# Maxima of the softmax turned on VectorE: neighbouring queries for the maximum pass of a pooled attention kernel

## The chip, the core and the metric

The kernel runs on one of the eight cores of a Trainium2 chip. Five engines work beside each other, each on its own instruction queue: TensorE (PE; its weight loads are listed apart as PEld), VectorE (DVE), ScalarE (ACT), GpSimd (POOL) and SyncE (SP), which in this kernel issues nearly all DMAs. The metric is the device time of one execution in microseconds (us), lower is better; the time before is the median of three executions.

## The reference

Attention with pooled queries (pairs of neighbouring queries averaged: 1152 become 576) over 8 batches of 8 heads with 64 dimensions, then a second stage on the result, x:

```python
q_pool = q.reshape(B, H, S // 2, 2, D).mean(axis=3)
scores = scale * np.matmul(q_pool, k.transpose(0, 1, 3, 2))
scores = scores - np.max(scores, axis=-1, keepdims=True)
attn = np.exp(scores)
attn = attn / (np.sum(attn, axis=-1, keepdims=True) + 1e-09)
x = np.matmul(attn, v)          # then laid out as (B, S/2, H*D)
theta = x @ w_theta
zr, zi = x * np.cos(theta), x * np.sin(theta)
u = x + einsum('ts,bsd->btd', w_tok_r, zr) + einsum('ts,bsd->btd', w_tok_i, zi)
out = u + np.maximum(u @ w_ch, 0.0)
```

The change touches only the way from the scores to `np.max(scores)`.

## The kernel before, in words

The first part of the program does the attention, in 32 pairs of heads (two heads of 64 dimensions fill the 128 partitions), and takes some 865 us; the second part does the rest batch by batch. In the first part each pair goes through these steps, and the steps of neighbouring pairs are interleaved:

- `prep_t`, `prep_hi`, `prep_lo`: TensorE turns keys and pooled queries (`pt`), ScalarE writes the rounded value `hi`, VectorE the rest `lo`. Both tiles hold, along a partition, the keys in two blocks with the 576 queries between them, from column `Q0` on.
- `maxpass` (line 317): the maximum of the scores is taken from `hi` alone. For each of four groups of 128 queries (`j`) and three groups of 384 keys (`g`) two matmuls, one per head, write `pm`. Here the 128 *queries* are the stationary operand, which TensorE loads before each matmul, and the keys stream past. VectorE reduces `pm` to a column of the small tile `mx` (line 324). A group `j` holds the queries j, j+4, j+8, ...: its columns stand four elements apart in `hi`. So twelve pairs of `pm` matmuls belong to one pair of heads. The last 64 queries go through `max_tail` (`px`, `py`).
- `max_nm` (line 345) makes `nm`, 128 partitions by 9 columns, the negated maxima: four columns for each head, and one for the tail.
- `load_max` (lines 351 and 352): four DMAs write `nm` into one row per head of `nmr`. With the spaced groups, partition p holds queries 4p to 4p+3 in four neighbouring words, so that a DMA writes 128 pieces of four words, or 64 of one word, to one partition.
- `escore` (line 371): eight matmuls write scores minus maximum into `pe` (three products of `hi` and `lo`, and `nmr` times a row of ones), ScalarE takes the exponential into `pc` (line 374). There are 18 of these per pair of heads.
- `ssum` (line 383): POOL adds the `pc` tiles of a half into `ss`, seven adds for each of two halves. TensorE sums `ss` over partitions (`pns`, line 419) and multiplies `pc` with the values (`pa`, line 397). The `norm_` steps divide, and turn the result (`xb`).

PSUM is used as four slots of two banks that `pm`, `pe`, `pt`, `px`, `pa`, `pns` share in turn. Tiles `ss` have two buffers per half, `pc` fourteen in all. The order of the instructions on every engine is written out: each step has a position in a table (`MAX_AT`, `PLAN`, `PREP_AT`), steps are sorted by position, and every engine, SP among them, runs its own in exactly that order. An instruction waits only for its own inputs and buffers, but everything behind it on its engine waits with it.

Of the kernel before, what the change touches and what calls it, by code (L numbers as in the profile page):

```python
# [9 lines left out]
F32 = mybir.dt.float32  # L10
F32R = mybir.dt.float32r
# [3 lines left out]
ALU = mybir.AluOpType  # L15
AX = mybir.AxisListType
# [68 lines left out]
def pooled_attention_moe_kernel(  # L85
# [11 lines left out]
    nc = tc.nc  # L97
    P = 128
    B, H, S, D = k.shape
    SQ = S // 2  # L100
    DM = H * D
    HALF = SQ // 2
    HT = SQ % P
    KC = SQ
    KT = S // P
# [39 lines left out]
    def bank2(kind, name):  # L145
        n = min(range(SLOTS), key=lambda k: slots[k])
        work, engines, after = HOLD[kind]
        psum["slot"] = n
        clock["p"] = max(clock["p"], slots[n]) + work
        end = max([clock["p"] + 0.3] + [clock[e] for e in engines]) + after  # L150
        for e in engines:
            clock[e] = end
        slots[n] = end + 0.1
        return psum["now"][0].tile([P, 2, 512], F32, tag=f"b{n}", name=name, bufs=1)
# [45 lines left out]
    with ExitStack() as p1:  # L200
# [7 lines left out]
        nrm = p1.enter_context(tc.tile_pool(name="nrm", bufs=1))  # L208
        sml = p1.enter_context(tc.tile_pool(name="sml", bufs=2))

        nmrs = [nrm.tile([P, 5 * P], F32R, name=f"nmr_{n}") for n in range(2)]
        for n in range(2):
            nc.gpsimd.memset(nmrs[n].bitcast(F32), 0.0)
        tails = [opd.tile([P, P], F32R, name=f"tail_{n}", bufs=1) for n in range(2)]
        for n in range(2):
            nc.gpsimd.memset(tails[n].bitcast(F32), 0.0)
        oner = nrm.tile([P, P], F32R, name="oner")
        nc.gpsimd.memset(oner.bitcast(F32), 0.0)
        for a in (0, D):
# [2 lines left out]
        state = {}  # L222
# [39 lines left out]
        Q0 = 6 * P  # L262
# [45 lines left out]
        def maxpass(i):  # L308
            st = state[i]
            hi = st["hi"]  # L310
            mx = st["mx"] = sml.tile([P, KT, 3], F32, tag="mx", name=f"mx{i}")
            W = 3 * P
            for j in range(4):
                for g in range(3):
                    pm = bank2("pm", f"pm{i}_{j}{g}")
                    for h, hs in enumerate(HEADS):
                        nc.tensor.matmul(  # L317
                            pm[:, h, 0:W],
                            hi[hs, Q0 : Q0 + 4 * P].rearrange("d (p j) -> d j p", j=4)[:, j],
                            hi[hs, K0[3 * g] : K0[3 * g] + W],  # L320
                            start=True,
                            stop=True,
                        )
                    nc.vector.tensor_reduce(  # L324
                        mx[:, j : j + 5 : 4, g : g + 1], pm[:, :, 0:W], AX.X, ALU.max
                    )
                    yield
# [13 lines left out]

        def max_nm(i):
            st = state[i]
            nm = st["nm"] = sml.tile([P, KT], F32R, tag="nm", name=f"nm{i}")
            nc.vector.tensor_reduce(nm, st["mx"], AX.X, ALU.max, negate=True)  # L345

        def load_max(i):
            nmr, nm = state[i]["nmr"].bitcast(F32), state[i]["nm"].bitcast(F32)
            for h in range(2):
                row = nmr[h * D : h * D + 1]  # L350
                nc.sync.dma_start(row[:, 0 : 4 * P], nm[:, 4 * h : 4 * h + 4])
                nc.sync.dma_start(row[:, 4 * P : SQ], nm[h * HT : (h + 1) * HT, 8:9])

        def escore(i, u, kt):
            st = state[i]
# [306 lines left out]
        def plan(i):  # L662
# [10 lines left out]
            for n, (name, fn, args) in enumerate((  # L673
# [4 lines left out]
                if i >= (3, 3, 3, 2, 2, 2, 2, 2)[n]:  # L678
                    at(base + PREP_AT[name], 3, fn, *args)
            at(base + pl["load_max"], 7, load_max, i)  # L680
            at(base + pl["load_v"], 5, load_v, i)
            gen = maxpass(i)
            for n in (MAX_AT0, MAX_AT1, MAX_AT)[min(i, 2)]:
                at(base + n, 2, run, gen, 1)
            at(base + pl["max_nm"], 7, max_nm, i)
            for u in range(2):
                for kt in range(KT):
# [366 lines left out]
```

## Time and profile before

| what | value |
|---|---|
| median of three executions | 1321.58 us (1321.48 to 1322.57) |
| the profiled execution: its own time, its span | 1321.95 us, 1320.2 us |
| PE busy, share of the span | 1288.2 us, 98% |
| PEld busy | 1083.3 us, 82% |
| POOL busy | 895.4 us, 68% |
| DVE busy | 847.7 us, 64% |
| ACT busy | 665.7 us, 50% |

The span is the time from the first to the last instruction of the program; the execution's own time is 1.75 us longer. A share is an average over both parts of the program: in forty equal slices of the span, POOL stands at 8 tenths or more from the third to the 26th, which is the first part, and mostly at 2 to 3 tenths after them. TensorE's granted clock is at nine tenths or more of full in all but the first slice.

### The profile page before, as it was taken

To read this page: it belongs to the slowest core of one execution; us is meant where nothing else is said; L and a number is where in the kernel's file an instruction comes from. 1 tells how busy PE (TensorE), PEld (TensorE's weight loads), DVE (VectorE), ACT (ScalarE), POOL (GpSimd) and SP (SyncE) were. 2 spreads that over 40 slices of the span, in tenths; PEclk is the share of its full clock that TensorE was granted. 3 is DMA by queue.
4 is the path that set the end of the run, shared out by engine and by line. 5 is a ranking of instruction groups with operands and counts; after the bars stand their busy time and mean duration, and the time that the engine had idled before them with its cause. 6 is when DMAs were issued, how large, how long until landed. Compare 5 with 4: busy or idle time off the path is not lost.

```text
span 1320.2 us, 29458 instructions
## 1 busy us (share of the span) xinstructions
PE 1288.2 (98%) x11850; PEld 1083.3 (82%) x11850; DVE 847.7 (64%) x1151; ACT 665.7 (50%) x1162; POOL 895.4 (68%) x664
## 2 busy tenths in 40 slices
PE   5999999999999999999999999999999999999998
PEld 3877787778787778787777777678899999999997
DVE  6766777676767686776777686545555636647452
ACT  1555555556565656565656555454443433434430
POOL 1799899999898998889998988834333333232310
PEclk7999999999999999999999999999999999999999
DMA  5335444444444444434544423225515335154231
GB/s 131 102 95 139 106 122 116 117 127 117 119 116 130 112 119 118 122 104 117 134 116 119 119 69 96 70 82 131 101 29 100 53 74 111 26 97 78 52 46 37
DMA packets 283209, 131.05 MB, mean 99 GB/s; under 512 B 247024, under 2 KB 247152, under 8 KB 283072
## 3 DMA queue, kind: packets, MB, share of 16 engines
q1 hardware_dynamic: 282896, 128.71, 40.0%
q8 instruction: 93, 1.52, 0.5%
q0 software_dynamic: 176, 0.46, 0.1%
q14 instruction: 44, 0.36, 0.1%
HBM read 97.21 MB, written 30.70 MB: 97 GB/s over the span
## 4 chain that ended last, share of the span: by engine, by line
PE 89%; DVE 4%; ACT 3%; DMA 1%; issue 1%; POOL 1%; SPq 0%; POOLq 0%; ACTq 0%; DVEq 0%
PE pe L371 21%; PE pa L397 21%; PE py L874 15%; PE pm L317 8%; PE pr L913 7%; PE pth L786 7%; PE pt L277 4%; PE pns L419 3%; DVE mx L324 2%; PE px L334 1%; ACT pc L374 1%; ACT Z L843 1%; DMA kn<-in_k_dram 0%; DMA xn<-xbd 0%; PE pwt L600 0%
## 5 line engine op out<-in xcount | busy, mean ns | idle before, releaser
L383 POOL TENSOR_TENSOR ss<-ss,pc 128x576 f32<-128x576 f32 x376 | 548.5, 1459 | 33.0 <-ACT pc L374 7.7
L324 DVE TENSOR_REDUCE mx<-pm 128x2 f32<-128x768 f32 x384 | 358.4, 956 | 204.6 <-PE pm L317 204.5
L374 ACT ACTIVATE pc<-pe 128x576 f32<-128x576 f32 x576 | 344.7, 652 | 79.1 <-PE pe L371 64.2
L397 PE MATMUL pa<-pc,vn 128*64 128x288 f32 x2304 | 294.1, 409 | 0.0
L397 PEld LDWEIGHTS pa<-pc,vn 128*64 128x64 f32 x2304 | 160.1, 137 | 119.1 <-DVE nm L345 7.4
L874 PE MATMUL py<-wtk,Z 128*128 128x288 f32 x1728 | 233.4, 295 | 0.0
L874 PEld LDWEIGHTS py<-wtk,Z 128*128 128x128 f32 x1728 | 231.9, 189 | 1.3
L847 POOL TENSOR_TENSOR Z<-ab,Z 128x512 fp32r<-128x512 f32 x40 | 52.1, 1303 | 257.3 <-ACT Z L843 242.0
L317 PE MATMUL pm<-hi 64*128 64x384 f32 x768 | 174.0, 464 | 4.7 <-ACT hi L293 2.1
L371 PE MATMUL pe<-hi 64*128 64x288 f32 x1152 | 174.1, 296 | 2.9 <-ACT pc L374 1.7
L371 PE MATMUL pe<-nmr,oner 64*128 64x288 f32 x1152 | 172.2, 292 | 1.6 <-DMA nmr<-nm 1.6
L371 PE MATMUL pe<-lo,hi 64*128 64x288 f32 x1152 | 172.2, 293 | 0.0
L371 PE MATMUL pe<-hi,lo 64*128 64x288 f32 x1152 | 172.1, 293 | 0.0
L317 PEld LDWEIGHTS pm<-hi 64*128 64x128 f32 x768 | 118.2, 306 | 35.3 <-issue 26.0
L409 ACT COPY xu<-pa 128x288 f32<-128x288 f32 x64 | 25.5, 399 | 212.9 <-PE pa L397 212.9
L371 PEld LDWEIGHTS pe<-hi 64*128 64x128 f32 x1152 | 113.6, 192 | 7.2 <-ACT pc L374 2.6
L383 POOL TENSOR_TENSOR ss<-pc,pc 128x576 f32<-128x576 f32 x64 | 92.3, 1442 | 31.9 <-ACT pc L374 31.6
L371 PEld LDWEIGHTS pe<-nmr,oner 64*128 64x128 f32 x1152 | 110.6, 185 | 2.0 <-DMA nmr<-nm 1.9
L371 PEld LDWEIGHTS pe<-hi,lo 64*128 64x128 f32 x1152 | 110.2, 185 | 0.0
L371 PEld LDWEIGHTS pe<-lo,hi 64*128 64x128 f32 x1152 | 110.0, 185 | 0.0
L913 PEld LDWEIGHTS pr<-us,wch 128*128 128x128 f32 x768 | 104.2, 189 | 1.7
L913 PE MATMUL pr<-us,wch 128*128 128x288 f32 x768 | 105.1, 295 | 0.0
(99 smaller groups left out, 1499.5 us busy)
## 6 DMA issues: line engine op xcount, KB each, us to landing
qn<-in_q_dram SPq DMA_DIRECT2D x32, 576.0 KB
kn<-in_k_dram SPq DMA_DIRECT2D x64, 288.0 KB
vn<-in_v_dram SPq DMA_DIRECT2D x32, 576.0 KB
dn<-ro SPq DMA_DIRECT2D x64, 144.0 KB
xd<-xu SPq DMA_DIRECT2D x32, 288.0 KB
xbd<-xb SPq DMA_DIRECT2D x32, 288.0 KB
xT<-xd SPq DMA_DIRECT2D x8, 1152.0 KB
xn<-xbd SPq DMA_DIRECT2D x140, 64.0 KB
```

The source lines that it names most:

```text
L277: nc.tensor.transpose(out=pt[:, n, c : c + R], in_=src.rearrange("p h d -> p (h d)"), identity=ident[0:R, 0:R],)
L317: nc.tensor.matmul(pm[:, h, 0:W], hi[hs, Q0 : Q0 + 4 * P].rearrange("d (p j) -> d j p", j=4)[:, j], hi[hs, K0[3 * g] : K0[3 * g] + W], sta ...
L324: nc.vector.tensor_reduce(mx[:, j : j + 5 : 4, g : g + 1], pm[:, :, 0:W], AX.X, ALU.max)
L371: nc.tensor.matmul(pe[:, h, 0:HALF], w[hs], x[hs], start=(n == 0), stop=(n == 3))
L374: nc.scalar.activation(pcs[u, kt], pe[:, :, 0:HALF], AF.Exp, scale=SC)
L383: nc.gpsimd.tensor_tensor(st["ss", u], first, st["pc"][u, kt], ALU.add)
L397: nc.tensor.matmul(pa[hs, 0, 0:HALF], st["vn"][:, h, kt, :], st["pc"][u, kt][:, h, :], start=(kt == 0), stop=(kt == KT - 1),)
L419: nc.tensor.matmul(px[a : a + 32, 1, 0:HALF], ones, sets[u][n][:, h, :], start=(n == 0), stop=(n == len(sets[0]) - 1), tile_position=(0, a),)
L786: nc.tensor.matmul(th, xs[c][:, j * P : (j + 1) * P], ws[:, c], start=(n == 0), stop=(n == 11))
L847: engine("zlo", b).tensor_tensor(Z[1], t, Z[0].bitcast(F32), ALU.subtract)
L874: nc.tensor.matmul(st["py", c, u][:, 0:HALF], Z[zi][:, c * P : (c + 1) * P], wtk[wi][:, kw, u * HALF : (u + 1) * HALF], start=(i == 0 and ...
L913: nc.tensor.matmul(pr[u][:, 0:HALF], wch[wi][:, c, e * P : (e + 1) * P], st["us", ui][:, c, u * HALF : (u + 1) * HALF], start=(n == 0), st ...
```

## The change

Three things change. The groups of queries in `maxpass` are now 128 neighbouring ones (0 to 127, 128 to 255, ...), so that the stationary operand is a plain slice of `hi`. The column of a group then holds the maxima of neighbouring queries down the partitions, so `max_nm` writes the nine columns into a tile `nm` of 32 columns that is kept (single, cleared once at the start), and VectorE turns it in four 32x32 pieces into `nt`, nine rows of 128. And `load_max` copies rows of `nt`: four rows of 128 words, and one row of 64, per head. `nmr` is 64 columns narrower.

```diff
-        nmrs = [nrm.tile([P, 5 * P], F32R, name=f"nmr_{n}") for n in range(2)]
+        nmrs = [nrm.tile([P, SQ], F32R, name=f"nmr_{n}") for n in range(2)]
...
+        TB = 32
+        nm = nrm.tile([P, TB], F32, name="nm")
+        nc.vector.memset(nm, 0.0)
+        nt = nrm.tile([TB, P], F32, name="nt")
...
                         nc.tensor.matmul(
                             pm[:, h, 0:W],
-                            hi[hs, Q0 : Q0 + 4 * P].rearrange("d (p j) -> d j p", j=4)[:, j],
+                            hi[hs, Q0 + j * P : Q0 + (j + 1) * P],
                             hi[hs, K0[3 * g] : K0[3 * g] + W],
...
         def max_nm(i):
             st = state[i]
-            nm = st["nm"] = sml.tile([P, KT], F32R, tag="nm", name=f"nm{i}")
-            nc.vector.tensor_reduce(nm, st["mx"], AX.X, ALU.max, negate=True)
+            nc.vector.tensor_reduce(nm[:, 0:KT], st["mx"], AX.X, ALU.max, negate=True)
+            for g in range(0, P, TB):
+                nc.vector.transpose(nt[:, g : g + TB], nm[g : g + TB])
 
         def load_max(i):
-            nmr, nm = state[i]["nmr"].bitcast(F32), state[i]["nm"].bitcast(F32)
+            nmr = state[i]["nmr"].bitcast(F32)
             for h in range(2):
                 row = nmr[h * D : h * D + 1]
-                nc.sync.dma_start(row[:, 0 : 4 * P], nm[:, 4 * h : 4 * h + 4])
-                nc.sync.dma_start(row[:, 4 * P : SQ], nm[h * HT : (h + 1) * HT, 8:9])
+                nc.sync.dma_start(row[:, 0 : 4 * P], nt[4 * h : 4 * h + 4])
+                nc.sync.dma_start(row[:, 4 * P : SQ], nt[8:9, h * HT : (h + 1) * HT])
```

The order of instructions is the same on PE, ACT, POOL and SP; only VectorE's has new rows. On VectorE, in the middle of the first part (sixteenth pair of heads; the numbers after a name only tell buffers apart), the queue before reads:

```order
L324 TENSOR_REDUCE mx_5584<-pm_32_5914 128x2
L345 TENSOR_REDUCE nm_5943<-mx_5584 128x9
L468 TENSOR_TENSOR xu_5174<-xu_5174,dn_5777 128x576
L473 STREAM_TRANSPOSE xb_5948<-xu_5174 128x576
L304 TENSOR_TENSOR lo_5714<-pt_16_5918,hi_5713 128x960
```

and now:

```order
L328 TENSOR_REDUCE mx_5632<-pm_32_5962 128x2
L348 TENSOR_REDUCE nm<-mx_5632 128x9
L350 STREAM_TRANSPOSE nt<-nm 32x32 x4
L473 TENSOR_TENSOR xu_5219<-xu_5219,dn_5825 128x576
L478 STREAM_TRANSPOSE xb_5999<-xu_5219 128x576
L308 TENSOR_TENSOR lo_5762<-pt_16_5966,hi_5761 128x960
```

Four 32x32 pieces stand behind `nm` and ahead of the division and the `lo` of the next pair; nothing else moved. On SP, for the same pair of heads, the queue before reads (`rd` and `rc` are DMAs of the division, `qn` loads queries):

```order
L436 DMA rd_6031<-sm_5940 4x288
L351 DMA nmr_117<-nm_5943 1x128x4
L352 DMA nmr_117<-nm_5943 1x64x1
L351 DMA nmr_117<-nm_5943 1x128x4
L352 DMA nmr_117<-nm_5943 1x64x1
L442 DMA rc_6071<-rd_6031 128x9
```

and now:

```order
L441 DMA rd_6082<-sm_5988 4x288
L356 DMA nmr_117<-nt 1x4x128
L357 DMA nmr_117<-nt 1x16x4
L356 DMA nmr_117<-nt 1x4x128
L357 DMA nmr_117<-nt 1x16x4
L447 DMA rc_6122<-rd_6082 128x9
```

The four DMAs keep their places; only their source and the pieces that they move are others.

## Rows read from the trace of the kernel before

**Rows 1.** Page, busy us (share) xinstructions; and the chain that ended last, by line.
```profile
PE 1288.2 (98%) x11850; PEld 1083.3 (82%) x11850; DVE 847.7 (64%) x1151; ACT 665.7 (50%) x1162; POOL 895.4 (68%) x664
...
PE pe L371 21%; PE pa L397 21%; PE py L874 15%; PE pm L317 8%; PE pr L913 7%; PE pth L786 7%; PE pt L277 4%; PE pns L419 3%; DVE mx L324 2%; PE px L334 1%; ACT pc L374 1%; ACT Z L843 1%; DMA kn<-in_k_dram 0%; DMA xn<-xbd 0%; PE pwt L600 0%
```
**Rows 2.** Page, groups: form xcount | busy us, mean ns of one | idle before.
```profile
L317 PE MATMUL pm<-hi 64*128 64x384 f32 x768 | 174.0, 464 | 4.7 <-ACT hi L293 2.1
...
L317 PEld LDWEIGHTS pm<-hi 64*128 64x128 f32 x768 | 118.2, 306 | 35.3 <-issue 26.0
...
L371 PEld LDWEIGHTS pe<-hi,lo 64*128 64x128 f32 x1152 | 110.2, 185 | 0.0
```
**Rows 3.** Timeline of PE: start us, us, instruction, xcount, idle before.
```profile
401.73 0.29 PE L371 MATMUL pe<-nmr,oner 64*128 64x288 f32 x2
401.86 0.44 PE L317 MATMUL pm<-hi 64*128 64x384 f32 x2
402.14 0.30 PE L371 MATMUL pe<-hi 64*128 64x288 f32 x2
...
414.99 0.56 PE L317 MATMUL pm<-hi 64*128 64x384 f32 x2
415.39 0.30 PE L371 MATMUL pe<-hi 64*128 64x288 f32 x2
```
**Rows 4.** Groups of PE by form, two widths of the same kind of matmul.
```profile
L874 PE MATMUL py<-wtk,Z 128*128 128x288 f32 x1728 | 233.4, 295 | 0.0
...
L786 PE MATMUL pth<-wth,xh 128*128 128x512 f32 x288 | 74.1, 400 | 2.2 <-DVE r L812 2.1
```
**Rows 5.** Waits of the weight loads: us in total, times, longest us.
```profile
PEld pm L317 <- issue: 26.0, 60, 0.4
```
**Rows 6.** Timeline of PE, a score tile directly behind the value matmuls.
```profile
832.62 0.40 PE L371 MATMUL pe<-hi 64*128 64x288 f32 x2
832.85 0.29 PE L371 MATMUL pe<-lo,hi 64*128 64x288 f32 x2
```
**Rows 7.** Timeline of VectorE, the first pair's maxima.
```profile
13.21 10.46 DVE L324 TENSOR_REDUCE mx<-pm 128x2 f32<-128x768 f32 x12
```
**Rows 8.** Windows from one pns to a next: us, busy PE PEld DVE ACT POOL.
```profile
252.79:278.90 26.11, 26.03 (x276) 20.40 (x276) 18.33 (x24) 14.79 (x26) 25.48 (x19) 1.00 0.46 124
278.90:305.18 26.28, 26.12 (x276) 20.50 (x276) 20.75 (x25) 15.15 (x27) 24.68 (x19) 1.00 0.51 126
305.18:331.49 26.31, 26.31 (x281) 20.93 (x281) 18.64 (x21) 14.75 (x26) 23.16 (x18) 1.00 0.39 103
...
409.37:436.04 26.67, 26.11 (x276) 20.50 (x276) 17.55 (x22) 15.48 (x28) 25.30 (x20) 1.00 0.43 122
...
sum 757.66, PE 754.01 PEld 595.23 DVE 545.92 ACT 438.61 POOL 695.25; mean PE 26.00 PEld 20.53 DVE 18.82 ACT 15.12 POOL 23.97
```
**Rows 9.** Groups of VectorE by form.
```profile
L473 DVE STREAM_TRANSPOSE xb<-xu 128x576 f32<-128x576 f32 x32 | 24.9, 779 | 2.1 <-DMA xbd<-xb 1.0
...
L345 DVE TENSOR_REDUCE nm<-mx 128x9 fp32r<-128x27 f32 x32 | 5.7, 180 | 0.9
...
L125 DVE MEMSET eps<- 128x1 f32 x1 | 0.1, 59 | 0.0
```
**Rows 10.** Timeline of VectorE behind two nm.
```profile
311.41 0.96 DVE L324 TENSOR_REDUCE mx<-pm 128x2 f32<-128x768 f32 x1 [1.02 <-PE pm L317]
...
410.09 0.18 DVE L345 TENSOR_REDUCE nm<-mx 128x9 fp32r<-128x27 f32 x1
...
415.60 1.82 DVE L324 TENSOR_REDUCE mx<-pm 128x2 f32<-128x768 f32 x2 [1.95 <-PE pm L317]
```
**Rows 11.** Timeline of SP: issue of two DMAs of maxima.
```profile
29.92 0.61 SPq L352 DMA_DIRECT2D nmr<-nm  x1
...
411.85 0.53 SPq L351 DMA_DIRECT2D nmr<-nm  x1
```
**Rows 12.** Timeline of PE, the first use of the maxima.
```profile
31.43 0.94 PE L371 MATMUL pe<-nmr,oner 64*128 64x288 f32 x2 [1.59 <-DMA nmr<-nm]
```

## The prediction

> **What bounds the kernel now.** I read the page first, for shares and the chain; then the groups, for what one instruction costs; then TensorE's timeline in the middle of the first part, for what a matmul costs in its place; then windows by pair of heads, for who is next behind TensorE; last the waits, VectorE's and SP's. TensorE is busy 98% of the span, and the chain that ended last runs over PE lines nearly throughout [rows 1]. In the first part it hardly waits: the 29 pairs of heads from 69.33 to 826.99 us take 757.66 us, and TensorE is busy 754.01 of them [rows 8]. So what shortens TensorE's work there shortens the kernel, until another engine is late. That would be POOL, busy 695.25 us of the same stretch, 92%; VectorE has 72%, ScalarE 58%.
>
> The line that the change touches, `pm`, stands out in one respect. Its weight load, 64 rows by 128 columns, takes 306 ns; that of `pe` has the same shape, reads the same tile `hi`, and takes 185 [rows 2]. The difference that I see in the code is that the columns of the first stand four elements apart. Loads run under the matmuls before them, so one must see whether the 121 ns come out. They do: `pm` starts 0.13 us behind a `pe` (401.73 to 401.86), which is what any `pe` takes, and the next `pe` comes only 0.28 us later [rows 3].
>
> **The change part by part.** *The load.* What a `pm` pair (two matmuls, one per head, side by side) would take if its load were hidden: 0.13 us as a `pe` of 288 columns, plus 96 more columns. A matmul of 512 columns takes 400 ns and one of 288 takes 295 [rows 4], 0.47 ns a column, so 45 ns more, 0.175 us together. It takes 0.28: the gain is 0.105 us. This also fits the 0.121 us that the load itself should lose, less what was hidden.
>
> Sixty of the `pm` pairs start behind a `pa`, where the load finds nothing to hide under: it is 60 times that the load engine stood idle before them [rows 5]. There `pm` to next `pe` takes 0.40 us [rows 3]. A `pe` directly behind a `pa` takes 0.23 [rows 6], and with 0.045 for the columns 0.275: the gain is 0.125.
>
> There are 768 matmuls, 384 pairs [rows 2]. The twelve of the first pair of heads gain nothing: VectorE's twelve maxima stand end to end for 10.46 us there and set the pace [rows 7]. I also leave out the next three, in the same start-up. So 309 x 0.105 = 32.4 us, and 60 x 0.125 = 7.5 us: TensorE's work gets 39.9 us shorter, 1.3 us for each pair of heads. All of it lies on the chain, if nothing takes its place. Its lower bound is 0 (a rival below); above it I allow nothing, since the `pm` would then be faster than its columns.
>
> *What is late next.* The repeating pattern is seven pairs of heads long, and POOL's share differs in it, since the preparation of the weights for the second part comes in some of them. In the window 252.79 to 278.90 POOL is busy 25.48 of 26.11 us, and the 0.63 us between its instructions look like all that it can't use. TensorE would then want 26.03 - 1.3 = 24.73. POOL can't follow: the pair lasts 0.75 us longer (POOL busy without a break) to 1.38 (with its breaks). The next window wants 26.12 - 1.3 = 24.82 against POOL's 24.68, even; the third wants 25.01 against 23.16, so POOL catches up; that of 409.37 wants 24.81 against 25.30, 0.49 to 1.12 us short, but behind lighter pairs [rows 8]. The sums say that POOL just fits on average: 695.25 + 29 x 0.63 = 713.5 us against TensorE's 754.01 - 29 x 1.3 = 716.3. Only the unevenness costs. Lower bound 0, if two buffers of `ss` and fourteen of `pc` level it all; upper bound, nothing levelled, 1.38 + 0.49 + 1.12 = 2.99 us in seven pairs, 12.4 us over 29. I take 1.2 us in seven, the one heaviest pair nearly whole, since the others have a lighter one ahead: 5 us.
>
> *The pieces.* VectorE gets 4 x 32 = 128 turns of 32x32. The trace has none so small. The bounds are 59 ns, the shortest instruction on VectorE, and 779 ns, a whole turn of 576 columns [rows 9]; by columns a piece has an eighteenth of that one, and `nm` itself, 27 columns in, takes 180. I take 0.1 us, nearest to the small rows: 0.4 us for a pair of heads, and some 0.1 for the wait on `nm`. Behind them on VectorE stand the division of an older pair, its turn, the `lo` of the next pair, and the first maxima of that pair. There VectorE waits for TensorE anyway, 1.95 us at 415.60 and 1.02 at 311.41 [rows 10]; so 0.5 us cost nothing, and `lo` is first read several us later. If that idle were gone, the price would be 0.5 x 31 = 16 us.
>
> The first piece waits for `nm`, and for the DMAs that read `nt` for the pair before, since `nt` is single. Those were issued some 26 us earlier, one pair of heads, so I count nothing.
>
> *The DMAs.* The four keep their place in SP's queue. `nm` ends at 410.27 [rows 10] and the first of them is issued at 411.85 [rows 11], behind other DMAs: the half microsecond of turning falls into a wait that is there. Only in the first pair of heads does TensorE wait for them, 1.59 us until 31.43 [rows 12], the last being issued at 29.92 to 30.53 [rows 11]. Fewer pieces could shorten this by anything from 0 to 1.6 us, a later `nt` could lengthen it by 0.5; I take 0.5 us less.
>
> Sum: -39.9 + 5 + 0 - 0.5 = -35.4 us, against the profiled execution's 1321.95 us (span 1320.2): 1286.5. The median of the runs is 0.4 lower, 1321.58: **1286 us**.
>
> **The rivals.** *POOL as the bound throughout.* If each pair keeps POOL's breaks, and its adds don't level out over the buffers, 12.4 us go instead of 5, and 1321.6 - 39.9 + 12.4 = 1294 us; with TensorE's slots freed a little later too, up to 1300. For it speaks the 92%; against it that a pair in three has over 1.5 us to spare. Chance 0.20. *POOL costs nothing:* 1321.6 - 39.9 - 0.5, some 1281 us, with all of the first wait gone 1280. For it speak the averages above; against it the window in which POOL is full. Chance 0.10.
>
> *The load doesn't get shorter.* Then nothing changes on TensorE, and the pieces are covered: 1322 us, within 0.2% of before. For it speaks only that the 306 ns come with `pm` and could hang on something else in it, such as its 384 moving columns; against it that the load of `pe`, same tile and shape, has 185. Chance 0.05. The Trainium skill, "TensorE: Matmul & The Clock Gate", section "LDWEIGHTS (loading the stationary operand)", says that a load takes as long as its number of columns, which by its words would give both loads the same time and the change no gain. The 306 and 185 ns of two loads of 128 columns [rows 2] speak against it here. "SBUF — State Buffer" of the Trainium skill, section "Door 1: The DMA port swizzle (why `[64,N]` ≈ `[32,N]`)", has reads lose speed where each falls into another line of 16 bytes; a step of four words does just that, and by that rule the gain is the one worked out above.
>
> *VectorE's queue behind `nm`*, the case that is slower. Four pieces of d us stand ahead of `lo` and of the next maxima. Past 1.95 / 4 = 0.49 us a piece they eat the idle of VectorE behind them, the slots of `pm` come free later, and TensorE waits; past (1.95 + 1.3) / 4 = 0.81 us they eat more than the load gives. The whole turn of 576 columns takes 0.779 [rows 9], so this needs pieces no cheaper than that and a load that gains little: without gain 31 x (3.12 - 1.95) = 36 us, 1358 us. Chance 0.02.
>
> **How the numbers follow.** Forecast 0.63, POOL throughout 0.20, POOL free 0.10, load unchanged 0.05, VectorE 0.02. The range takes in the free case's 1280 and most of POOL's case: 1279 to 1298. About 0.2%, 2.6 us, is what a measurement of this kernel can tell from no change. Faster by more: the first three, 0.93, and a little of the fourth, where the first wait gets shorter, 0.94; within: 0.03; slower: 0.03, the last case and a share of the fourth with costly pieces.
>
> **What would show it.** The load of `pm` near 185 ns, and 0.17 to 0.18 us from a `pm` to the next `pe` in the middle of the first part; the 29 pairs of heads some 34 us shorter, with POOL busy 96% or more of them, and TensorE idle where POOL's `ss` or a `pc` buffer is late, most in the windows with the weights' preparation; pieces below 0.2 us, with VectorE still idle behind them; the second part as long as before. I am wrong in the load if it stays near 306, in the price of POOL if TensorE is idle for less than 2 us or more than 12 in that stretch beyond what it is now, and in the cover if VectorE's idle ahead of the next maxima is gone.

## The result, and the profile after

The changed kernel takes 1302.34 us (median of four runs, 1300.03 to 1302.37) against 1321.8 of the kernel before beside it: ratio 0.9848, 95% interval 0.9831 to 0.9865. So it is 19.5 us faster, and not the 35.4 us that were forecast. 1302.34 lies above the whole range of 1279 to 1298. Timed a second time, beside two of the experiments below, it took 1302.12 (1301.99 to 1302.93), ratio 0.9858 (0.9841 to 0.9874).

The page of its profile, busy time (share of the span) xinstructions, and the chain that ended last by line; these answer to [rows 1].

```profile
PE 1264.4 (97%) x11850; PEld 1044.2 (80%) x11850; DVE 878.0 (68%) x1280; ACT 669.5 (51%) x1162; POOL 896.2 (69%) x664
...
PE pe L376 22%; PE pa L402 21%; PE py L879 15%; PE pr L918 8%; PE pth L791 7%; PE pm L321 5%; PE pt L281 4%; PE pns L424 3%; DVE mx L328 2%; ACT pc L379 1%; PE px L338 1%; DVE lo L308 1%; DVE xu L473 1%; ACT Z L848 1%; DVE wf L547 1%
```

Line `pm` has gone from 8% of the chain to 5%, `pe` stays on top, and three lines of VectorE, `lo`, `xu` and `wf` (preparation of the weights), are new in it with 1% each. TensorE's busy time has dropped by 23.8 us. By shares alone nothing has come up behind it.

The groups of the page, as in [rows 2]: busy, mean ns of one | idle before.

```profile
L376 PE MATMUL pe<-hi 64*128 64x288 f32 x1152 | 185.6, 316 | 8.1 <-DVE lo L308 2.7
L376 PE MATMUL pe<-nmr,oner 64*128 64x288 f32 x1152 | 173.0, 293 | 1.0 <-DMA nmr<-nt 1.0
L376 PE MATMUL pe<-lo,hi 64*128 64x288 f32 x1152 | 172.0, 292 | 0.0
...
L321 PE MATMUL pm<-hi 64*128 64x384 f32 x768 | 137.5, 368 | 4.4 <-ACT hi L297 2.1
...
L376 PEld LDWEIGHTS pe<-hi 64*128 64x128 f32 x1152 | 109.8, 185 | 23.3 <-DVE lo L308 4.5
...
L321 PEld LDWEIGHTS pm<-hi 64*128 64x128 f32 x768 | 73.8, 188 | 37.9 <-issue 25.1
```

The weight load of `pm` takes 188 ns, as that of `pe`; it was 306. The matmuls of `pm` take 368 instead of 464. So the load did what was forecast. The row that betrays the loss is the first: of the four products that make a score tile, the first one, `pe<-hi`, has a mean of 316 ns, and the other three 292 or 293. Before, it was 296, and the others 292 or 293:

```profile
L371 PE MATMUL pe<-hi 64*128 64x288 f32 x1152 | 174.1, 296 | 2.9 <-ACT pc L374 1.7
```

Its weight load in the changed kernel is as short as theirs. Something lengthens the first matmul of a tile, and it counts as busy time, not as idle.

The timeline of PE at the place of [rows 3], in the middle of the first part: start, us, instruction.

```profile
392.99 0.29 PE L376 MATMUL pe<-nmr,oner 64*128 64x288 f32 x2
393.12 0.34 PE L321 MATMUL pm<-hi 64*128 64x384 f32 x2
393.29 0.30 PE L376 MATMUL pe<-hi 64*128 64x288 f32 x2
...
393.69 0.29 PE L376 MATMUL pe<-nmr,oner 64*128 64x288 f32 x2
393.82 0.39 PE L376 MATMUL pe<-hi 64*128 64x288 f32 x2
394.05 0.29 PE L376 MATMUL pe<-lo,hi 64*128 64x288 f32 x2
```

From the `pm` to the next `pe` it is 0.17 us (393.12 to 393.29), where it was 0.28. But at the second score tile behind this `pm`, the `pe<-hi` at 393.82 lasts 0.39, and the next product comes 0.23 us behind it instead of 0.13. That is 0.1 us lost, as much as the `pm` has won. The same place before:

```profile
402.54 0.30 PE L371 MATMUL pe<-nmr,oner 64*128 64x288 f32 x2
402.67 0.30 PE L371 MATMUL pe<-hi 64*128 64x288 f32 x2
402.81 0.29 PE L371 MATMUL pe<-lo,hi 64*128 64x288 f32 x2
```

The weight loads of the changed kernel around that tile:

```profile
393.56 0.19 PEld L376 LDWEIGHTS pe<-nmr,oner 64*128 64x128 f32 x2
393.81 0.19 PEld L376 LDWEIGHTS pe<-hi 64*128 64x128 f32 x2
393.92 0.19 PEld L376 LDWEIGHTS pe<-lo,hi 64*128 64x128 f32 x2
```

In the first and the third row a load starts 0.13 us ahead of its own matmul (393.69 and 394.05) and lies under the matmuls before it. The second one should start at 393.69 and starts at 393.81, beside its own matmul. It waited, and with nothing to lie under it its time comes out. The Trainium skill ("TensorE: Matmul & The Clock Gate", section "Architectural detail: the array is 16× 32×32, not 1× 128×128") says that TensorE's queue can pull loads ahead of matmuls in flight; the row at 393.56 agrees, and that at 393.81 shows a load that was not pulled ahead.

What it waited for is seen on VectorE:

```profile
392.80 1.83 DVE L328 TENSOR_REDUCE mx<-pm 128x2 f32<-128x768 f32 x2
```

Two maxima stand here in one row; the first starts at 392.80, takes 0.96 and ends at 393.76, 0.05 us before that load starts. It frees the PSUM slot of the `pm` that started at 392.31, four slots back, and the tile at 393.82 is the next in that slot. The written order of the program says the same, here in two of its rows near a `pm 12`:

```
L376 MATMUL pe_02_5834<-hi_4974 128x288 [waits Activation_49]
...
L376 MATMUL pe_03_5848<-hi_4974 128x288 [waits DVE_49]
```

Half of the 18 score tiles follow a score tile in their slot and wait for ScalarE's exponential (the first row's tile follows a `pa` and waits for ScalarE's copy). The fourth, eighth, tenth, 14th and 18th of a pair of heads follow a `pm` and wait for VectorE, and the 12th follows a `pt` (each in 26 or 27 of 27 pairs of heads). For the eighth and the fourth the times can be read one by one, counted from the start of the `pm` that had the slot (medians of 27 pairs of heads, us, from the starts and ends in the timelines of PE, PEld and VectorE):

| | kernel | reduction ends | load of the new tile starts | its matmul starts | load ahead of its matmul |
|---|---|---|---|---|---|
| 8th tile | before | 1.44 | 1.49 | 1.61 | 0.12 |
| 8th tile | after | 1.34 | 1.39 | 1.40 | 0.01 |
| 4th tile | before | 1.57 | 1.62 | 1.74 | 0.12 |
| 4th tile | after | 1.45 | 1.50 | 1.51 | 0.01 |

The load starts 0.054 us behind the end of the reduction, in both kernels: it waits for VectorE, and did so before. But before, the four slots took 1.61 us to come round (two `pm` with two score tiles between them), and the load still had its 0.12 us ahead of its matmul. In the changed kernel the `pm` shorten the round by 0.21 us, and the reduction's end by 0.10 only. So the load comes out from under the matmuls: the tile's first product waits for it, which is the 0.1 us.

Over 27 pairs of heads, what the second product of a tile came later than 0.133 us behind the first, summed by place of the tile (worked out from the starts in TensorE's timeline, us; the changed kernel by its second profile):

| tile of the pair of heads | 4th | 8th | 10th | 12th | 14th | 18th | all 18 |
|---|---|---|---|---|---|---|---|
| before | 0.07 | 0.09 | 0.01 | 0.21 | -0.02 | 0.38 | 1.12 |
| after | 2.66 | 2.12 | 0.46 | 0.94 | 1.59 | 2.48 | 10.93 |

The windows from one `pns` to a next answer to [rows 8]: us, busy time of PE, PEld, DVE, ACT, POOL.

```profile
247.55:273.68 26.13, 25.28 (x277) 19.08 (x276) 20.47 (x29) 14.87 (x26) 25.50 (x20) 1.00 0.45 124
...
sum 739.72, PE 731.28 PEld 558.59 DVE 571.75 ACT 442.01 POOL 696.09; mean PE 25.22 PEld 19.26 DVE 19.72 ACT 15.24 POOL 24.00
```

The 29 pairs of heads take 739.72 us instead of 757.66, 17.9 less (the forecast was 34). TensorE is idle for 8.4 us of them, before 3.65. What it waited for in this stretch, us in total, times, longest:

```profile
PE pe L376 <- DVE lo L308: 2.7, 4, 1.0
PE pe L376 <- ACT pc L379: 2.1, 4, 0.7
PE pe L376 <- DVE mx L328: 1.9, 4, 0.5
```

POOL does not stand in it, though in the window of 247.55 it is busy 25.50 of 26.13 us. VectorE does, 4.6 us, twice: for a late `lo`, and for maxima. One of the four late `lo`, on VectorE:

```profile
95.23 0.18 DVE L348 TENSOR_REDUCE nm<-mx 128x9 f32<-128x27 f32 x1
95.44 0.84 DVE L350 STREAM_TRANSPOSE nt<-nm 32x32 f32<-32x32 f32 x4
96.32 1.80 DVE L473 TENSOR_TENSOR xu<-xu,dn 128x576 f32<-128x576 f32 x1
98.16 0.78 DVE L478 STREAM_TRANSPOSE xb<-xu 128x576 f32<-128x576 f32 x1
98.86 1.12 DVE L308 TENSOR_TENSOR lo<-pt,hi 128x960 fp32r<-128x960 f32 x1
```

and on TensorE:

```profile
100.03 0.40 PE L376 MATMUL pe<-hi 64*128 64x288 f32 x2 [1.03 <-DVE lo L308]
```

At the same place before:

```profile
94.95 0.87 DVE L542 SCALAR_TENSOR_TENSOR wf<-raw,wf 128x513 uint32<-128x513 uint32 x1
96.82 0.88 DVE L468 TENSOR_TENSOR xu<-xu,dn 128x576 f32<-128x576 f32 x1
```

The four turns take 0.84 us together, with `nm` ahead and the division and its turn behind, and `lo` ends after TensorE wants it. But the division takes 1.80 us here and took 0.88 before, and a `wf` among the last maxima takes 1.40 instead of 0.87. In both kernels the division takes anything from 0.74 to over 3 us; what sets that stays open, so the lateness is not the turns' alone.

### The profile page after: what moved, and what is told of

The parts are those of the page before. It is cut to its first block, busy times and chain, and to the rows that moved or that the text cites. A ratio compares the mean times of both kernels' runs of the same rounds, so it can differ in the third digit from the quotient of the medians.

```text
span 1300.6 us, 29614 instructions
## 1 busy us (share of the span) xinstructions
PE 1264.4 (97%) x11850; PEld 1044.2 (80%) x11850; DVE 878.0 (68%) x1280; ACT 669.5 (51%) x1162; POOL 896.2 (69%) x664
## 4 chain that ended last, share of the span: by engine, by line
PE 86%; DVE 6%; ACT 3%; issue 2%; DMA 1%; POOL 1%; SPq 0%; POOLq 0%; ACTq 0%; DVEq 0%
PE pe L376 22%; PE pa L402 21%; PE py L879 15%; PE pr L918 8%; PE pth L791 7%; PE pm L321 5%; PE pt L281 4%; PE pns L424 3%; DVE mx L328 2%; ACT pc L379 1%; PE px L338 1%; DVE lo L308 1%; DVE xu L473 1%; ACT Z L848 1%; DVE wf L547 1%
## 5 line engine op out<-in xcount | busy, mean ns | idle before, releaser
L379 ACT ACTIVATE pc<-pe 128x576 f32<-128x576 f32 x576 | 348.4, 652 | 62.7 <-PE pe L376 39.5
L376 PE MATMUL pe<-hi 64*128 64x288 f32 x1152 | 185.6, 316 | 8.1 <-DVE lo L308 2.7
L321 PE MATMUL pm<-hi 64*128 64x384 f32 x768 | 137.5, 368 | 4.4 <-ACT hi L297 2.1
L376 PEld LDWEIGHTS pe<-hi 64*128 64x128 f32 x1152 | 109.8, 185 | 23.3 <-DVE lo L308 4.5
L321 PEld LDWEIGHTS pm<-hi 64*128 64x128 f32 x768 | 73.8, 188 | 37.9 <-issue 25.1
```

Of the source, the lines that this page charges most:

```text
L321: nc.tensor.matmul(pm[:, h, 0:W], hi[hs, Q0 + j * P : Q0 + (j + 1) * P], hi[hs, K0[3 * g] : K0[3 * g] + W], start=True, stop=True,)
L376: nc.tensor.matmul(pe[:, h, 0:HALF], w[hs], x[hs], start=(n == 0), stop=(n == 3))
L379: nc.scalar.activation(pcs[u, kt], pe[:, :, 0:HALF], AF.Exp, scale=SC)
```

## The experiments

Theory *slots*: VectorE's hold on the slot of a `pm` is longer than the new round, and each such wait lays a weight load bare. Rivals: POOL as forecast; the turns and the queue behind `nm`; VectorE's whole work, wherever it stands. Each kernel was timed beside the kernel before, and the ratio is to that. "Stretch" is the 29 pairs of heads, 757.66 us before and 739.45 in the changed kernel's second profile.

**Half the work of a maximum (e1_half).** The changed kernel with

```diff
-    mx[:, j : j + 5 : 4, g : g + 1], pm[:, :, 0:W], AX.X, ALU.max
+    mx[:, j : j + 5 : 4, g : g + 1], pm[:, :, 0 : W // 2], AX.X, ALU.max
```

> The changed kernel, but VectorE reduces only the first half of the 384 columns of each pm (the maxima are over half of the keys; the matmuls are unchanged). A pm is reduced some 0.4 us sooner. Theory slots (a pm's PSUM slot comes round 1.42 to 1.52 us after the pm began, before VectorE has reduced it, and each such wait also uncovers a weight load, some 0.1 us): the stalls at the starts of the fourth, eighth and last score tile of a pair of heads go, some 10 to 14 us less than the changed kernel's 1302, so 1288 to 1292. Theory POOL (its adds set the pace nearly everywhere): no change, 1300 to 1303. Theory pieces (the 0.85 us of turning makes VectorE late behind nm): part of it, 1294 to 1298.

1280.6 us, 0.9687 (0.9672 to 0.9701), 21.7 us below the changed kernel. The groups and the sum of its windows:

```profile
L328 DVE TENSOR_REDUCE mx<-pm 128x2 f32<-128x384 f32 x384 | 210.4, 558 | 263.4 <-PE pm L321 254.6
L376 PE MATMUL pe<-hi 64*128 64x288 f32 x1152 | 175.2, 296 | 4.6 <-ACT pc L379 2.5
...
sum 724.61, PE 719.03 PEld 555.97 DVE 435.87 ACT 438.31 POOL 697.13; mean PE 24.79 PEld 19.17 DVE 15.03 ACT 15.11 POOL 24.04
```

The maxima take 558 ns instead of 956, `pe<-hi` is back at 296, and the stretch is 14.8 us shorter, with POOL's work as it was. The theory *slots* expected 10 to 14 us in all; it is 21.7. VectorE it is, then, and with more than was expected. Some 6 us more come from the start-up, where the first pair's twelve maxima stand end to end [rows 7] and are halved too: the first `pns` starts at 62.14 instead of 68.85.

The window in which POOL was to be the bound looked like its case: 26.13 us with POOL busy 25.50, next to the 26.11 of the prediction's case with all of POOL's breaks (25.48 + 0.63). In e1_half, with all of POOL's adds, the same window takes 24.53:

```profile
238.50:263.03 24.53, 24.53 (x276) 19.03 (x276) 15.15 (x29) 14.78 (x26) 23.98 (x19) 1.00 0.48 132
```

So POOL's work moves into the neighbouring windows when TensorE is not held up by VectorE.

**One seventh of POOL's adds left out (e3_pool)**, and **both together (e5_half_pool)**. The add of the fourth `pc` of each half is left out:

```diff
-            if kt == 0 or kt >= (TAIL if i < NPAIR - 1 else TAIL_LAST):
+            if kt in (0, 4) or kt >= (TAIL if i < NPAIR - 1 else TAIL_LAST):
```

> The changed kernel with one of the seven adds of each half left out on POOL (the sums lack one key tile): 2.9 us less POOL work for each pair of heads, nothing else changed. Theory POOL: 8 to 15 us less than 1302, so 1287 to 1294. Theory slots: 0 to 3 us less, 1299 to 1302, and the 0.1 us stalls at the fourth, eighth and last score tile stay. Theory pieces: the same as slots.

> The changed kernel with both cuts: VectorE reduces half of each pm (maxima over half of the keys), POOL leaves out one of seven adds (the sums lack one key tile). If slots and POOL together hold the whole missing gain, TensorE's work alone is left: 1282 to 1286. If something else holds a part (the pieces, the order, the clock), it stays above 1290.

e3_pool: 1297.99 us, 0.9819 (0.9805 to 0.9834); stretch 737.35, 2.1 us shorter; `pe<-hi` stays at 315 ns. The whole kernel is 4.4 us faster; most of the rest lies behind the stretch, where the granted clock stays at 1.00 in this profile and falls in the changed kernel's (last section). e5_half_pool: 1279.5, 0.9677 (0.9661 to 0.9693), stretch 723.07, 1.5 us below that of e1_half.

```profile
sum 723.07, PE 718.73 PEld 555.98 DVE 438.47 ACT 438.55 POOL 612.56; mean PE 24.78 PEld 19.17 DVE 15.12 ACT 15.12 POOL 21.12
```

With 85 us less work POOL gives back 1.5 to 2.1 us of the stretch. It was not POOL that took 16. With both engines relieved the stretch is 34.6 us shorter than before, near the 37.7 that the forecast prices of the load give for it (348 steps); 3.7 of the 34.6 are what half the maxima are worth without the shorter load, as the next run shows.

**The kernel before with half the maxima (e6_bhalf).** The same edit as in e1_half, with the slow load.

> The kernel before with the half reduce (maxima over half of the keys). Here a pm's slot comes round 1.63 us after its start, later than VectorE has reduced it. Theory slots: nothing to gain, 1319 to 1322. If VectorE's work or its reading of PSUM slows TensorE in general: as much as in e1, 1300 or less.

1312.34 us, 0.9941 (0.9925 to 0.9958). Of its 8.4 us some 5 lie in the start-up (first `pns` at 64.12 instead of 69.33); the stretch takes 753.92, 3.7 us less. Neither expectation holds: the theory *slots* had nothing to gain here, its rival 20 us or more. The same relief is worth 14.8 us with the short load and 3.7 with the long one. So the cost of VectorE's hold is for the most part not one that the kernel always had: the change called it up.

**Slot time against VectorE's sum of work (e8_fill, e10_fill2).** Half maxima free the slot early, but also give VectorE half its time back. Both kernels take half the maxima and put an unread reduction of a constant behind each, so that VectorE is done with the slot after 0.56 us instead of 0.96, and goes on working:

```diff
-    mx[:, j : j + 5 : 4, g : g + 1], pm[:, :, 0:W], AX.X, ALU.max
+    mx[:, j : j + 5 : 4, g : g + 1], pm[:, :, 0 : W // 2], AX.X, ALU.max
+)
+nc.vector.tensor_reduce(
+    fl, ident.rearrange("p (o c) -> p o c", o=1).broadcast_to([P, 3, P]), AX.X, ALU.max
```

e10_fill2 has 2 instead of 3 in the last line, 256 words.

> The changed kernel with the half reduce of e1 (maxima over half of the keys), and behind each of these a filler on VectorE: a maximum over 384 words of the identity, whose result nobody reads. So VectorE is about as busy as in the changed kernel, but each pm is reduced, and its slot free, some 0.4 us sooner. Theory slots (the time until a slot is free decides): most of e1's gain stays, 1281 to 1289. Rival, VectorE's total work decides: 1298 to 1304.

> The changed kernel with maxima over half the keys, and behind each an unread reduction of 256 words, so that VectorE's work in a pair of heads is that of the changed kernel again (about 0.56 + 0.40 us for a pm) while a pm's slot is free after half the time. Left out: the maxima over the other half of the keys. Theory slots (the time that VectorE holds a pm's slot): no 0.1 us starts at tiles 3, 7, 13 and 17, and most of the gain of the half maxima stays, 1281 to 1291 us. Rival total (VectorE's sum of work, or what it keeps from others, whatever the slots): as the changed kernel, 1298 to 1303 us.

e8_fill: 1295.95 us, 0.9813 (0.9798 to 0.9827), stretch 734.33. e10_fill2: 1290.87, 0.9773 (0.9758 to 0.9787), stretch 729.55. The first lies between what the two theories expected, the second at the edge of what *slots* did. e10_fill2's groups and sum, and that of e8_fill:

```profile
L329 DVE TENSOR_REDUCE mx<-pm 128x2 f32<-128x384 f32 x384 | 213.4, 556 | 170.7 <-PE pm L322 170.3
L380 PE MATMUL pe<-hi 64*128 64x288 f32 x1152 | 175.9, 298 | 7.5 <-DVE lo L309 3.1
...
sum 729.55, PE 720.78 PEld 555.98 DVE 546.39 ACT 438.19 POOL 697.99; mean PE 24.85 PEld 19.17 DVE 18.84 ACT 15.11 POOL 24.07
```

```profile
sum 734.33, PE 722.58 PEld 555.98 DVE 594.04 ACT 438.29 POOL 696.49; mean PE 24.92 PEld 19.17 DVE 20.48 ACT 15.11 POOL 24.02
```

and the tile of the timeline above, in e10_fill2:

```profile
388.81 0.30 PE L380 MATMUL pe<-nmr,oner 64*128 64x288 f32 x2
388.95 0.30 PE L380 MATMUL pe<-hi 64*128 64x288 f32 x2
389.08 0.29 PE L380 MATMUL pe<-lo,hi 64*128 64x288 f32 x2
```

The 0.1 us are gone here and in nearly all such tiles: at the eighth the reduction of the `pm` now ends 0.95 us after that `pm` started, the round is 1.42, and the load stands 0.17 us ahead of its matmul. The sum over 27 pairs of heads falls from 10.93 to 2.16 us. Of the changed kernel's second profile to this one, the step from a score tile's first product to its second gets shorter by 5.4 us behind a `pm` and by 4.2 behind another score tile, and the stretch by 9.9: they are the same microseconds. VectorE's sum was not hit exactly: 546 us in the stretch here and 594 in e8_fill, around the changed kernel's 571. On the line between the two, 571 us would give some 732, an estimate: at equal work the slots alone are worth 7 us or a little more. The other 5 to 7, down to e1_half's 724.61, follow VectorE's sum of work. For the most part they are the waits for a late `lo`, 3.1 us in e10_fill2 and 0.7 in e1_half, and for late maxima, 1.4 and 0.3. So both theories on VectorE hold a part, the slots about half or more.

**One number of the order (e11_order).** Nothing is left out; `pm 10` moves behind the 18th score tile, so that three tiles instead of two and a `pm` stand between `pm 02` and the next user of its slot:

```diff
-MAX_AT = (-25.047, -24.524, -21.303, -19.913, -17.966, ...
+MAX_AT = (-25.047, -24.524, -21.303, -18.95, -17.966, ...
```

> The changed kernel with one number of MAX_AT changed (-19.913 to -18.95): pm 10 stands behind the last pe of a pair of heads instead of ahead of it, so that three pe instead of two pe and a pm stand between pm 02 and the next user of its slot (1.77 us instead of 1.42). Nothing is left out. Theory slots: the 0.1 us starts at tile 17 (2.4 us in the stretch, with waits behind them 2.8) go, 1298 to 1300 us if pm 10 and pm 11, now closer together, cost nothing in their place. Rival: the 0.1 us are put down to the wrong cause and belong to tile 17 itself (its place behind a pm): then they stay or move with the pm, 1302 us.

1300.93 us, 0.9847 (0.9832 to 0.9861), beside the changed kernel's own run (e13_after):

> The changed kernel as it is, beside the other two on the same chip, so that differences of 2 us can be told: 1300 to 1302.4 us, 0.984 to 0.985 of before by every theory. If the profiled execution has no fall of the granted clock near 831 us, the 29 pairs of heads take about 2.9 us less than in the first profile of this kernel (739.7).

1302.12 us, 0.9858 (0.9841 to 0.9874). Its profile has a fall of the granted clock near 832 us too (last section), so the condition of that expectation's second sentence is not met; and the fall lies behind the stretch, which ends at 808.30. The stretch of e11_order takes 739.09 against 739.45. The 18th tile, and what comes soon behind, in e11_order:

```profile
409.97 0.30 PE L376 MATMUL pe<-hi 64*128 64x288 f32 x2
410.10 0.30 PE L376 MATMUL pe<-lo,hi 64*128 64x288 f32 x2
...
411.40 0.35 PE L321 MATMUL pm<-hi 64*128 64x384 f32 x2
411.85 0.87 PE L281 MATMUL pt<-ident,kn 128*128 128x128 f32 x6
...
411.85 0.20 PEld L281 LDWEIGHTS pt<-ident,kn 128*128 128x128 f32 x2 [0.36 <-ACT pc L379]
```

The sum of the 18th tiles falls from 2.48 to 0.09 us, by the order alone: the loss is tied to the slot, not to the tile. But the `pt` behind `pm 11` now starts 0.45 us behind it (411.40 to 411.85), where the median was 0.27. With the new order this `pt` follows the 18th score tile in its slot, and its load waits for ScalarE, whose exponential of that tile ends at 411.80 (the last row). So the wait has moved to another slot, and to another engine that holds it. In 28 such places it costs 4.8 us, and the step behind gives 1.6 back. The intervals of the two kernels overlap: no gain that can be told.

**The load alone (e9_load).** The kernel before with the plain slice and nothing else; its maxima, written as before, go to other queries than they belong to.

```diff
-    hi[hs, Q0 : Q0 + 4 * P].rearrange("d (p j) -> d j p", j=4)[:, j],
+    hi[hs, Q0 + j * P : Q0 + (j + 1) * P],
```

> The kernel before with the neighbouring queries alone: the plain slice as stationary operand, no pieces, the scattering DMAs as before (the maxima land at other queries than their own). Theory slots: the load is nearly all of the change, and it runs into the same stalls: 1296 to 1301, some 3 us under the changed kernel, since VectorE is spared the pieces. If the pieces took the missing gain: 1284 to 1290.

1300.34 us, 0.9846 (0.9832 to 0.9861).

```profile
L371 PE MATMUL pe<-hi 64*128 64x288 f32 x1152 | 184.8, 315 | 6.3 <-DVE mx L324 3.7
L317 PE MATMUL pm<-hi 64*128 64x384 f32 x768 | 137.6, 369 | 5.0 <-ACT hi L293 2.1
L317 PEld LDWEIGHTS pm<-hi 64*128 64x128 f32 x768 | 73.6, 188 | 38.8 <-issue 25.6
```

One line of the change brings its whole gain, and the same loss in `pe<-hi`. It was to end some 3 us under the changed kernel and ends 2.0 under it. By this the step of four words is the cause of the 306 ns, and the turns are not what takes the gain.

**The turns alone (e4_pieces)**: the kernel before, with the four turns into an unread tile (`nm`, here `nw`, is one kept tile as in the changed kernel); and **one turn of four (e2_one)**: the changed kernel without the other three, the rest of `nt` being zero.

```diff
+    nc.vector.tensor_reduce(nw[:, 0:KT], st["mx"], AX.X, ALU.max, negate=True)
+    for g in range(0, P, TB):
+        nc.vector.transpose(nt[:, g : g + TB], nw[g : g + TB])
```

> The kernel before with the four 32x32 turns added behind nm, into a tile that nobody reads; spaced queries and scattering DMAs as before. The turns take 0.85 us of VectorE for each pair of heads. If VectorE's idle behind nm covers them, as the prediction had it: 1320 to 1323. If not, up to 26 us more, 1348; theory slots expects 0 to 3 us, since the slots come round 0.1 us later in this kernel.

```diff
-            for g in range(0, P, TB):
+            for g in range(0, TB, TB):
```

> The changed kernel with one of the four 32x32 turns of a pair of heads, the other three left out (their maxima stay zero). VectorE has 0.64 us less for each pair of heads, all of it behind nm. Theory pieces: most of the missing gain comes back, 1287 to 1294. Theory slots: only the stalls just behind nm can shrink, 1299 to 1302. Theory POOL: no change, 1301 to 1303.

e4_pieces: 1323.76 us, 1.0019 (1.0010 to 1.0028), 2.5 us slower than before. e2_one: 1299.55, 0.9833 (0.9816 to 0.9849), 2.8 below the changed kernel, with intervals that overlap. In the stretch e4_pieces takes 759.33 us, 1.7 more than before; e9_load, without turns, takes 738.44, 1.0 less than the changed kernel; and e2_one takes 739.77, no less than the changed kernel. What its profile gains lies outside: 1.7 us ahead of the stretch and 2.6 behind it, where its granted clock stays at 1.00 (last section). So the turns cost some 1 to 2.5 us, not nothing. Without them the score tiles' waits for a late `lo` go (2.5 us in the changed kernel, 0 in e9_load, 0.7 in e2_one), but waits for late maxima take their place, 3.7 and 3.8 us instead of 1.9.

## Why the prediction was wrong

*The load* was right in cause, and in size for the single step. 188 ns, and 0.175 us from `pm` to `pe`; the median step fell by 0.102 us behind a score tile (0.105 forecast) and by 0.120 behind a `pa` (0.125). The Trainium skill's column rule, weighed as a rival ("TensorE: Matmul & The Clock Gate", section "LDWEIGHTS (loading the stationary operand)"), has 306 ns for one load of 128 columns and 188 for another against it, with the same columns in e9_load; its rule on lines of 16 bytes ("SBUF — State Buffer", section "Door 1: The DMA port swizzle (why `[64,N]` ≈ `[32,N]`)") agrees in direction with both. Not all steps got it, though. In 29 of the stretch's 348 a second `pm` follows the first directly with a `pt` or the weights' turn behind; these went from 0.369 to 0.347 and 0.338 us only, as the next one waits for a slot. Summed over the 348 steps in TensorE's timeline the gain is 29.7 us, where the forecast prices give 37.7 (39.9 for all 369). So a fifth of the sum did not come; with half the maxima (e1_half) it is 35.6, so most of that is VectorE's doing too.

*What is late next* is the step that failed. The prediction looked for the engine with the least time to spare in a window, found POOL with 92%, and gave it 5 us. It passed over VectorE with 72%. In the runs POOL is worth 1.5 to 2.1 us of the stretch, and VectorE about 15 (e1_half), of which 3.7 were there before the change (e6_bhalf). POOL's share was to reach 96% of the stretch, and is 94%. What decides is not how much VectorE does in 26 us, but how soon it is done with one `pm` after that `pm` started, against how soon the ring of four slots comes round. The kernel before stood at the edge: 1.44 us against a round of 1.61, with the load just hidden between them. Both were to be had ahead: [rows 3] give the round (two steps of 0.28 and two tiles of 0.53) and the 0.44 us until a `pm` is done, [rows 10] the 0.96 us of a reduction. POOL's rival had "TensorE's slots freed a little later too, up to 1300" in half a sentence, without a price, and as POOL's doing.

The give-back by the same timelines, in the stretch: the step from a score tile's first product to its second is 10.8 us longer in all (5.7 behind a `pm`, 5.1 behind another score tile), and the other steps 0.7. So 29.7 gained less 11.5 is 18.2, which is the stretch's difference (757.66 to 739.45); 5 was forecast for the 11.5. The spans differ by 19.7: 0.5 us lies ahead of the stretch and 1.0 behind it.

*Its idle time as cover.* That VectorE waits for TensorE behind `nm` [rows 10] was read as room: 1.95 and 1.02 us. It is there in the changed kernel too, 1.44 us at 406.38. Idle time in one place does not help a `pm` elsewhere: VectorE can't take a maximum ahead of time. And it is not there in every pair of heads, as the late `lo` at 100.03 shows.

*The pieces* were mis-sized and then priced at nothing: 200 ns each, not 100. Four take 0.84 us in a pair of heads, within the bounds of 0.059 to 0.779 us each. 31 x 0.84 is 26 us of VectorE's time, of which some 1 to 2.5 come out at the end (e9_load, e4_pieces). The fourth rival's mechanism, then, at a small price.

*The DMAs.* The first wait for the maxima is 1.0 us instead of 1.59 [rows 12], 0.6 less, near the 0.5 forecast. But the issue did not get cheaper with fewer pieces: it takes as long as in [rows 11]. And from the end of the last issue to TensorE's start it is 0.73 us (29.85 to 30.58) instead of 0.90 (30.53 to 31.43): fewer pieces can be worth 0.2 us, the rest is that the last issue came earlier. That the figure fits is luck.

```profile
28.64 0.63 SPq L356 DMA_DIRECT2D nmr<-nt  x1
29.32 0.53 SPq L357 DMA_DIRECT2D nmr<-nt  x1
...
30.58 0.99 PE L376 MATMUL pe<-nmr,oner 64*128 64x288 f32 x2 [1.01 <-DMA nmr<-nt]
```

*What would make it wrong*: it said, if TensorE's idle time in the stretch grew by under 2 or over 12 us. It grew by 4.8, inside the bounds, and for other reasons. Most of the loss did not show as idle. 10.8 us of it stood in busy time, in one product of four, and a test on idle time could not see that. The Trainium skill ("Perfetto Trace Analysis", section "Identifying the Most-Contended Engine") warns that the busy share of matmuls is no good measure of the distance to the limit; here 97% busy hid some 10 us of waiting.

Left open: how the 5 to 7 us that follow VectorE's sum of work divide between a late `lo`, late maxima and the turns; what sets the time of the division; and whether any order of the twelve `pm` avoids these waits. Of the 37 tiles that a pair of heads puts into the four slots, 12 are `pm`, so that two in one round can't be avoided everywhere. One place was tried.

## What to carry to other kernels

Before counting a shorter step on the busiest engine as gain, work out for each buffer that it cycles through how long the round takes now and then, and how soon the consumer gives one back, from start to release; a consumer that is idle a quarter of its time can still be late every time. Compare the mean of the first instruction into a buffer with that of its like behind it: a wait of 0.1 us hides in busy time, and is seen as 316 beside 292 ns. And a weight load is free only as long as its matmul need not wait.

## What the runs showed of the hardware

- A load of 64 rows by 128 columns takes 306 ns where its columns stand four words apart, and 188 where they are neighbours (e9_load, that edit alone).
- A turn of 32 by 32 on VectorE takes 200 ns, and four of them 0.84 us; the large turn, 18 times as many columns, takes 779 [rows 9], 43 ns for each 32 columns. So most of the 200 does not go with the columns.

```profile
L350 DVE STREAM_TRANSPOSE nt<-nm 32x32 f32<-32x32 f32 x128 | 25.6, 200 | 2.5
```

- A weight load waits for the PSUM slot of its matmul: at the fourth and eighth tile it starts 0.054 us after the reduction that frees the slot, in both kernels and all 27 pairs of heads, and never ahead of it. A slot that is free when the matmul is due, but not a load earlier, costs 0.1 us.
- Near 828 us TensorE waits 2.79 us for POOL's last `ss` of the first part. From 831.5 to 840 its granted clock is then 0.65 in the first profile and 0.80 in the second, that is, part of the time at 1.2 GHz instead of 2.4; in e9_load, after a wait of 2.5 us, it is 1.00. The 36 value matmuls there take 6.42 us in the first profile and 4.52 in e9_load, and the `pns` ahead of them 2.14 and 1.17: the fall costs 2.9 us in the first profile, and 1.6 in the second (5.36 and 1.97). The kernel before has such a fall too (0.83 from 846 to 856), so the main comparison is hardly touched. But e2_one and e3_pool have none there in their profiles, and differences of 2 to 3 us between whole kernels can be this; the stretch ends ahead of it.
